# The first layer's weight tiles move from ahead of the working buffers in SBUF to behind them

## The chip, the cores and the metric

The kernel runs on one core of one Trainium2 chip. The metric is the device time of one execution in microseconds (us); for several executions the median is given. TensorE is PE in the profile, its weight loads stand apart as PEld; VectorE is DVE, ScalarE is ACT, GpSimd is POOL, and SyncE (SP) issues most of the DMAs.

## The reference

A dynamic convolution is followed by two feed-forward layers, all in float32, on 2 x 4096 tokens of 192 channels:

```python
w = softmax(weight_gen)                              # 8 heads, 7 taps for each token
x = einsum('bshk,bskhg->bshg', w, windows_of_7(x))   # 24 channels in a head
x = leaky(x.reshape(8192, 192) @ w_in1) @ w_out1     # 192 -> 2048 -> 192, leaky = max(0.01 h, h)
out = relu(x @ w_in2) ** 2 @ w_out2                  # 192 -> 2048 -> 192
```

## The kernel before, in words

**Tiling and order.** The tokens go in 16 blocks (tb) of 512. A phase is one layer l on one block. The five phases (0,0) to (0,4) come first, then (1,0), (0,5), (1,1), (0,6) and so on in turn up to (0,15), and last (1,11) to (1,15) of the second layer alone (L679 to L683). A phase has eight steps j, each for 256 of the 2048 hidden channels. So there are 256 steps, 128 of each layer. In a step TensorE runs `mm1(l, tb, j)` and then `mm2` of the step before the last one (LAG = 2): in the first two steps of a phase, `mm2` still belongs to the phase before, mostly to the other layer.

**The matmuls.** Values and weights are split in a high and a low float32r part, and the products high x high, high x low and low x high are added. Every matmul takes 64 partitions of contraction and 512 columns; two of them, one on partitions 0 to 63 and one on 64 to 127 (`HALVES`), are issued one behind the other and run side by side. `mm1` (L550) is 18 matmuls, nine such pairs: weights `wi0h`, `wi0l` (layer 0) or `wi1h`, `wi1l` (layer 1), moving tiles `xah`, `xbh`, `xsh`, `xal`, `xbl`, `xsl`. `mm2` (L592) is 20 matmuls, ten pairs: weights `wo0` or `wo1` (the trace calls both `wo`), moving tiles `gh` and `gl`, sums in the PSUM tiles `pa` and `pb`. A step thus has 19 pairs. The instructions of the two layers have the same shapes and the same waits.

**Other engines.** After `mm1`, ScalarE makes `gh` and `g` from PSUM (layer 0: two Prelu, L567 and L568, both read from PSUM; layer 1: a Relu from PSUM and two Square, L570 to L572), and VectorE makes `gl = g - gh` (L575). At a phase's end `total` (L613, L616) adds up the PSUM sums, and only then may the next phase's `mm2` write them. VectorE also does the convolution (`local_sum`, L472 and L484) ahead of a layer 0 phase, and at the start it decodes both layers' weights out of the words that lie in HBM (`piece`, L291 to L344).

**The planner.** `Plan.issue` writes out the order of each engine's operations from their costs and priorities. It knows tiles as rings of buffers, and nothing of addresses.

**Where tiles lie.** Pools are laid one behind the other in each SBUF partition in the order in which they are opened. Sizes follow from the tiles' shapes (bytes of one partition); places are counted from the start of `wi0h`:

| pool | what | bytes | place before |
|---|---|---|---|
| `const` | `ident`, `perm`, `warm`, then `wi0h`, `wi0l` (12,288 each), `wo0` (24,576) | 49,152 for layer 0's weights | 0 to 49,152 |
| `sb` | all working buffers; moving tiles of matmuls are `x..` (three rings of six tiles, 2,048 each), `gh`, `gl` (4,096 each) | 113,280 | 49,152 to 162,432 |
| `sg`, later `const2` | staging of layer 0's weights; in the same place, once that is done, layer 1's `wi1h`, `wi1l`, `wo1` | 49,152 | 162,432 to 211,584 |

Inside `sb`, the first `x` tile lies 25,216 bytes from the pool's start, the first `gh` 37,504, the first `gl` 53,888; all the moving tiles lie a multiple of 512 bytes from one another. One weight load takes 512 bytes of each partition, at a multiple of 512 bytes from the start of its layer's weights.

Of the kernel before, what the change touches and what calls it, by code (L numbers as in the profile page):

```python
# [141 lines left out]
def kernel(  # L142
# [42 lines left out]

    const = ctx.enter_context(tc.tile_pool(name="const", bufs=1))
    sb = ctx.enter_context(tc.tile_pool(name="sb", bufs=2))
    dram = ctx.enter_context(tc.tile_pool(name="dram", bufs=2, space=bass.MemoryType.DRAM))
    ps = ctx.enter_context(tc.tile_pool(name="ps", bufs=2, space=bass.MemoryType.PSUM))

# [27 lines left out]
    def weight_tiles(pool, l):  # L218
        wi.append({k: pool.tile([P, 3, NPR, P], F32R, name=f"wi{l}{k}") for k in "hl"})
        wo.append(pool.tile([P, NFC, 2 * D], F32R, name=f"wo{l}"))  # L220

    warm = const.tile([P, 1], F32, name="warm")
    weight_tiles(const, 0)
    wi_b = [[None] * NPR for _ in range(2)]
    wo_b = [[None] * NPR for _ in range(2)]
    SW = 2 * 3 * P
# [541 lines left out]
```

## Time and profile before

| what | value |
|---|---|
| median of 3 runs | 1188.23 us (1186.67 to 1189.9) |
| the profiled execution: its own time | 1187.0 us |
| its span, first to last instruction | 1185.2 us |
| mean granted clock of TensorE in it | 0.991 |
| busy: PE, PEld | 96%, 78% of the span |
| busy: ACT, DVE | 63%, 61% |

The profile shows one execution. Busy shares say little here by themselves; starts of consecutive matmuls, read from the timeline, say how long a step takes. A phase or a step is measured from the start of its first `mm1` matmul to that of the next.

### The profile page before, as it was taken

The page shows a single profiled execution, that of the slowest core. Times are in us where ns is not written, and L with a number is a line of the kernel's source. Part 1 is how long each engine was busy: PE and PEld are TensorE (multiplying, and loading weights), DVE is VectorE, ACT ScalarE, POOL GpSimd, SP SyncE. Part 2 cuts the span into 40 slices and gives each one's busy share as a digit, 9 for nine tenths or more (in the row PEclk, how much of TensorE's full clock was granted, in tenths as well). Part 3 has the DMA queues.
Part 4 walks back from the last instruction along what each step waited for, and adds up shares of the span by engine and source line. Part 5 has one row for each costly group of instructions (what it writes and reads, how often), then busy time and mean ns, then how long its engine had stood idle before and what let it go on. Part 6 is the DMA issues. An engine that isn't in the chain of part 4 may idle for free.

```text
span 1185.2 us, 22999 instructions
## 1 busy us (share of the span) xinstructions
PE 1137.3 (96%) x9748; PEld 929.3 (78%) x9748; DVE 725.5 (61%) x871; ACT 749.0 (63%) x830; POOL 15.9 (1%) x20
## 2 busy tenths in 40 slices
PE   2699999999999999999999999999999999999997
PEld 1479887888888888888888888888888888888885
DVE  7999999848465474745648475564846543344333
ACT  2555566574756748575674857657575675777774
POOL 0210000000000000000000000000000000000000
PEclk9799999999999999999999999999999999999999
DMA  8954646051512214142131513214151231121111
GB/s 185 221 105 105 158 129 171 14 136 19 148 20 79 70 42 127 19 124 44 57 93 37 131 19 105 60 33 121 22 146 19 86 80 45 56 63 37 19 19 18
DMA packets 112798, 94.29 MB, mean 80 GB/s; under 512 B 59644, under 2 KB 89114, under 8 KB 112696
## 3 DMA queue, kind: packets, MB, share of 16 engines
q1 hardware_dynamic: 108712, 87.99, 29.6%
q0 software_dynamic: 3792, 4.72, 2.5%
q8 instruction: 76, 1.25, 0.5%
q14 instruction: 26, 0.21, 0.1%
q10 hardware_dynamic: 192, 0.11, 0.0%
HBM read 50.06 MB, written 20.19 MB: 59 GB/s over the span
## 4 chain that ended last, share of the span: by engine, by line
PE 91%; DVE 6%; issue 1%; ACT 1%; DMA 1%; SPq 0%; POOL 0%; DVEq 0%; POOLq 0%; ACTq 0%
PE ph L550 43%; PE pa L592 29%; PE pb L592 19%; DVE gl L575 1%; DVE tmp L472 1%; DVE att L484 1%; DVE wa L302 1%; DVE wu L312 0%; DVE wu L308 0%; DVE wa L296 0%; DVE wo L344 0%; DMA xc<-in_x_dram 0%; ACT gh L567 0%; ACT wu L291 0%; DMA bw<-ob 0%
## 5 line engine op out<-in xcount | busy, mean ns | idle before, releaser
L575 DVE TENSOR_TENSOR gl<-g,gh 128x1024 fp32r<-128x1024 f32 x256 | 312.8, 1223 | 389.9 <-ACT g L572 293.1
L567 ACT ACTIVATE gh<-ph 128x1024 fp32r<-128x1024 f32 x128 | 131.6, 1028 | 262.8 <-PE ph L550 262.8
L592 PE MATMUL pa<-gh,wo 64*128 64x512 f32 x2048 | 280.9, 392 | 2.6 <-DVE s L616 2.0
L592 PEld LDWEIGHTS pa<-gh,wo 64*128 64x128 f32 x2048 | 194.2, 185 | 48.7 <-DVE oa L616 3.7
L570 ACT ACTIVATE g<-ph 128x1024 f32<-128x1024 f32 x128 | 131.7, 1029 | 120.6 <-PE ph L550 120.6
L592 PE MATMUL pa<-gl,wo 64*128 64x512 f32 x1024 | 160.7, 390 | 0.0
L592 PE MATMUL pb<-gh,wo 64*128 64x512 f32 x1024 | 160.4, 389 | 0.3 <-DVE wo L344 0.3
L592 PE MATMUL pb<-gl,wo 64*128 64x512 f32 x1024 | 160.5, 389 | 0.0
L571 ACT ACTIVATE gh<-g 128x1024 fp32r<-128x1024 f32 x128 | 135.8, 1061 | 4.0
L572 ACT ACTIVATE g<-g 128x1024 f32<-128x1024 f32 x128 | 136.0, 1062 | 3.5
L568 ACT ACTIVATE g<-ph 128x1024 f32<-128x1024 f32 x128 | 130.6, 1020 | 0.0
L592 PEld LDWEIGHTS pb<-gh,wo 64*128 64x128 f32 x1024 | 97.7, 185 | 21.3 <-DVE wo L344 0.7
L592 PEld LDWEIGHTS pb<-gl,wo 64*128 64x128 f32 x1024 | 97.7, 185 | 20.8
L592 PEld LDWEIGHTS pa<-gl,wo 64*128 64x128 f32 x1024 | 97.5, 184 | 20.9 <-DVE gl L575 0.4
L472 DVE TENSOR_TENSOR tmp<-xc,wg 128x768 f32<-128x768 f32 x96 | 91.1, 950 | 0.0
L484 DVE TENSOR_TENSOR att<-att,tmp 128x768 f32<-128x768 f32 x91 | 86.9, 955 | 1.7
L550 PE MATMUL ph<-xah,wi0h 64*128 64x512 f32 x256 | 53.0, 403 | 8.3 <-ACT wi0h L334 8.3
L550 PE MATMUL ph<-xah,wi0l 64*128 64x512 f32 x256 | 52.9, 402 | 3.3 <-DVE wi0l L344 3.3
L550 PE MATMUL ph<-xbl,wi0h 64*128 64x512 f32 x256 | 52.5, 399 | 1.0 <-DVE xbl L407 1.0
L550 PE MATMUL ph<-xsh,wi0l 64*128 64x512 f32 x256 | 52.8, 401 | 0.0
L550 PE MATMUL ph<-xsh,wi0h 64*128 64x512 f32 x256 | 52.5, 399 | 0.0
L550 PE MATMUL ph<-xbh,wi0l 64*128 64x512 f32 x256 | 52.5, 398 | 0.0
(98 smaller groups left out, 1462.2 us busy)
## 6 DMA issues: line engine op xcount, KB each, us to landing
xc<-in_x_dram SPq DMA_DIRECT2D x62, 240.0 KB, 4.5
xsh<-xah SPq DMA_DIRECT2D x60, 128.0 KB, 2.4
xsl<-xal SPq DMA_DIRECT2D x60, 128.0 KB, 2.4
raw<-in_moe_w_in_dram SPq DMA_DIRECT2D x32, 192.0 KB, 6.1
raw<-in_moe_w_out_dram SPq DMA_DIRECT2D x7, 768.0 KB, 5.1
sc<-xb SPq DMA_DIRECT2D x14, 384.0 KB, 2.3
ka<-s SPq DMA_DIRECT2D x16, 256.0 KB, 2.0
kb<-s SPq DMA_DIRECT2D x16, 256.0 KB, 3.2
```

Of the source, the lines that this page charges most:

```text
L302: lambda: nc.vector.scalar_tensor_tensor(I(wa), I(wu), SIGN, I(wa), op0=ALU.bitwise_and, op1=ALU.bitwise_or),
L472: nc.vector.tensor_tensor(dst, xk, wg.t[:, :, :, k : k + 1].to_broadcast([P, TB, H, G]), op=ALU.mult)
L484: lambda tmp=tmp: nc.vector.tensor_tensor(acc(), acc(), tmp.t, op=ALU.add),
L550: nc.tensor.matmul(ph.t[:, d, :], lhsT=w[HALVES[d], c, j, :], rhs=xs[s + hl].t[HALVES[d]], start=(i == 0), stop=(i == len(terms) - 1),)
L567: pl.op("ACT", W, pr, [ph], [gh], lambda: nc.scalar.activation(gh.t, ph.t, AF.Prelu, alpha=0.01))
L568: pl.op("ACT", W, pr, [ph], [g], lambda: nc.scalar.activation(g.t, ph.t, AF.Prelu, alpha=0.01))
L570: pl.op("ACT", W, pr, [ph], [g], lambda: nc.scalar.activation(g.t, ph.t, AF.Relu))
L571: pl.op("ACT", W, pr, [g], [gh], lambda: nc.scalar.activation(gh.t, g.t, AF.Square))
L572: pl.op("ACT", W, pr, [g], [g], lambda: nc.scalar.activation(g.t, g.t, AF.Square))
L575: lambda: nc.vector.tensor_tensor(gl.t, g.t, gh.t.bitcast(F32), op=ALU.subtract),
L592: nc.tensor.matmul(acc[d][w == "b"].t, lhsT=wt[:, {"ah": slice(0, P), "b": slice(P, 2 * P), "al": slice(2 * P, 3 * P)}[w]], rhs=g.t[HALVES ...
```

## The change

A pool `first` is opened behind `sb`, and layer 0's weight tiles are taken from it instead of from `const`. Nothing else is edited.

```diff
     const = ctx.enter_context(tc.tile_pool(name="const", bufs=1))
     sb = ctx.enter_context(tc.tile_pool(name="sb", bufs=2))
+    first = ctx.enter_context(tc.tile_pool(name="first", bufs=1))
     dram = ctx.enter_context(tc.tile_pool(name="dram", bufs=2, space=bass.MemoryType.DRAM))
...
     warm = const.tile([P, 1], F32, name="warm")
-    weight_tiles(const, 0)
+    weight_tiles(first, 0)
```

By the sizes above the working buffers then lie at 0 to 113,280, layer 0's weights at 113,280 to 162,432, and layer 1's weights where they were, at 162,432.

## Rows read from the trace of the kernel before

**Rows 1.** The page's part 1: busy us, share of the span, instructions.

```profile
PE 1137.3 (96%) x9748; PEld 929.3 (78%) x9748; DVE 725.5 (61%) x871; ACT 749.0 (63%) x830; POOL 15.9 (1%) x20
```

**Rows 2.** The page's part 4, the chain that ended last, by line.

```profile
PE ph L550 43%; PE pa L592 29%; PE pb L592 19%; DVE gl L575 1%; DVE tmp L472 1%; DVE att L484 1%; DVE wa L302 1%; DVE wu L312 0%; DVE wu L308 0%; DVE wa L296 0%; DVE wo L344 0%; DMA xc<-in_x_dram 0%; ACT gh L567 0%; ACT wu L291 0%; DMA bw<-ob 0%
```

**Rows 3.** Waits of PE from 82 us on: us in total, times, longest.

```profile
PE pa L592 <- DVE s L616: 2.0, 2, 1.1
PE ph L550 <- DVE xbl L407: 1.0, 1, 1.0
```

**Rows 4.** Windows: length, busy us (instructions) of PE, PEld, DVE, ACT, POOL, clock, DMA.

```profile
131.84:189.23 57.39, 57.39 (x496) 49.07 (x494) 53.42 (x65) 35.81 (x42) 0.00 (x0) 1.00 0.60 154
189.23:227.22 37.99, 35.95 (x307) 28.40 (x304) 35.28 (x47) 21.27 (x25) 0.00 (x0) 1.00 0.32 86
227.22:261.87 34.65, 34.65 (x306) 28.50 (x304) 18.84 (x21) 26.89 (x29) 0.00 (x0) 1.00 0.42 115
261.87:999.21 737.34, 737.34 (x6386) 598.37 (x6384) 427.89 (x496) 466.80 (x512) 0.00 (x0) 1.00 0.28 70
402.26:437.77 35.51, 35.51 (x306) 28.52 (x304) 27.13 (x33) 17.94 (x21) 0.00 (x0) 1.00 0.10 18
...
963.61:999.21 35.60, 35.60 (x306) 28.43 (x304) 14.67 (x16) 18.65 (x22) 0.00 (x0) 1.00 0.23 53
1033.86:1137.22 103.36, 103.36 (x915) 85.42 (x912) 42.22 (x45) 80.19 (x83) 0.00 (x0) 1.00 0.17 34
```

**Rows 5.** Line L550: duration of one matmul in ns, least, median, most; first and last start.

```profile
L550 PE MATMUL ph<-xsh,wi0l x256: 387/392/625, 28.8 to 996.4; 64*128 64x512 f32 x128
...
L550 PE MATMUL ph<-xah,wi1h x256: 386/386/394, 227.2 to 1167.4; 64*128 64x512 f32 x128
```

**Rows 6.** Timeline of PE: where `mm1` and `mm2` of four steps begin.

```profile
380.73 0.39 PE L550 MATMUL ph<-xah,wi1h 64*128 64x512 f32 x2
...
382.76 1.07 PE L592 MATMUL pa<-gh,wo 64*128 64x512 f32 x8
...
385.03 0.39 PE L550 MATMUL ph<-xah,wi1h 64*128 64x512 f32 x2
...
424.52 0.40 PE L550 MATMUL ph<-xah,wi0h 64*128 64x512 f32 x2
...
426.62 1.08 PE L592 MATMUL pa<-gh,wo 64*128 64x512 f32 x8
...
428.94 0.39 PE L550 MATMUL ph<-xah,wi0h 64*128 64x512 f32 x2
...
372.01 0.39 PE L550 MATMUL ph<-xah,wi1h 64*128 64x512 f32 x2
...
374.07 1.10 PE L592 MATMUL pa<-gh,wo 64*128 64x512 f32 x8
...
376.41 0.39 PE L550 MATMUL ph<-xah,wi1h 64*128 64x512 f32 x2
...
402.26 0.40 PE L550 MATMUL ph<-xah,wi0h 64*128 64x512 f32 x2
...
404.37 1.09 PE L592 MATMUL pa<-gh,wo 64*128 64x512 f32 x8
...
406.69 0.40 PE L550 MATMUL ph<-xah,wi0h 64*128 64x512 f32 x2
```

**Rows 7.** Timeline of the third step of a layer 0 phase.

```profile
411.12 0.41 PE L550 MATMUL ph<-xah,wi0h 64*128 64x512 f32 x2
411.12 0.19 PEld L550 LDWEIGHTS ph<-xbh,wi0h 64*128 64x128 f32 x2
...
413.27 0.53 PEld L592 LDWEIGHTS pa<-gh,wo 64*128 64x128 f32 x6 [0.34 <-DVE oa L616]
...
415.70 0.39 PE L550 MATMUL ph<-xah,wi0h 64*128 64x512 f32 x2
```

**Rows 8.** Waits of DVE from 82 to 227 us: us in total, times, longest.

```profile
DVE gl L575 <- PE pb L592: 5.9, 6, 1.9
```

## The prediction

> **What bounds the kernel now.** I read the page's busy shares first: PE is busy for 1137.3 of 1185.2 us [rows 1]. The chain that ended last says the same: L550 and L592 hold 91% of it [rows 2]. Third, the waits: from 82 us on PE waits for others for 3.0 us in three places [rows 3]; what comes before 82 us is the decoding of weights, where PE is not the bound. So from there to the end the time is the number of steps by the length of a step, and the only question is how long TensorE takes for a pair of matmuls.
>
> That length is not the same for the two layers. In the stretch of pure layer 1 at the end, 24 steps take 103.36 us [rows 4], 4.307 us each; divided by 19 pairs that is 226.7 ns for a pair. In the stretch of pure layer 0 near the start, 13 steps take 57.39 us, 4.415 us each or 232.3 ns for a pair. [...]
>
> The timeline says what it goes with [rows 6]. Where both weights are layer 1's, nine pairs of `mm1` take 2.03 us and ten of `mm2` 2.27. Where both are layer 0's, 2.10 and 2.32. In the second step of a layer 1 phase, `mm1` reads `wi1` and takes 2.06, while `mm2` still reads `wo0` and takes 2.34. So within one step, under the same ACT and DVE work, the length follows the weights that are read. One case fits less well: in the first step of a layer 0 phase `mm2` reads `wo1` and yet takes 2.32, after a slow `mm1`. In the case before, `mm1` was slower than 2.03 too after a slow `mm2`; I read both as a delay that takes some pairs to die out.
>
> Instructions and waits of the layers are alike, so what differs is where the weights lie. Every weight load begins while the matmul before it streams (both at 411.12 us [rows 7]): two reads of the same partitions at once. Layer 0's weights lie at multiples of 512 bytes from their start, the moving tiles at 49,152 + 25,216 = 145 x 512 + 128, so 128 bytes past such a multiple; layer 1's at 162,432 = 317 x 512 + 128, the same 128 past. In layer 1, all 256 matmuls of a kind take 386 to 394 ns, in layer 0 the median is 392 and none is below 387 [rows 5], whatever j or ring is read. So neither the row of the weight tile nor the ring of `x` counts. What remains is the place within 512 bytes, or the region of the partition as a whole. I take the first.
>
> **The change part by part.** No instruction is added, removed or moved in any queue, SP's and POOL's among them, and no wait: the planner does not see addresses, and `first` is opened as early as `const` was, so nothing waits for its space. The staging pool and layer 1's weights stay in their place. DMA issues and the cover of every DMA stay as they are. Two things move.
>
> Layer 0's weights go to 113,280 = 221 x 512 + 128, the moving tiles to 25,216 = 49 x 512 + 128. Now both layers' weights lie as layer 1's did to the moving tiles, and I price a pair at 226.7 ns throughout. No row shows weights in that region; the bounds are what rows 4 show, 226.7 and 232.3 ns, and nothing lower is known.
>
> The working buffers move down by 49,152 = 96 x 512 bytes. For layer 1's matmuls the place within 512 stays equal, so I take 0; the outer bound is that they take layer 0's 232.3 ns (a rival below).
>
> *The sum.* From 261.87 to 999.21 us there are 21 phases, 11 of layer 0 and 10 of layer 1, 168 steps in 737.34 us [rows 4]. At 4.307 us they take 723.6. Not all of the difference comes: in the third step of a layer 0 phase `mm2` waits until VectorE has read the old sums [rows 7]. That wait starts with the end of the `mm2` before, so a faster `mm1` only waits longer: 413.27 - 411.12 = 2.15 stays, against 2.04, and `mm2` at 2.43 keeps the 0.10 that it has over 2.32 to 2.34. So 0.21 x 11 = 2.3 us stay, and the stretch takes 725.9: **11.4 us gained**. The phase after it, like the one from 227.22 us (34.65 us against 8 x 4.307 = 34.46), gains 0.2, and that one 0.2. Between 189.23 and 227.22 us, about six of the eight steps are free of waits and gain 0.11 each, 0.7. The pure layer 1 steps gain 0.
>
> From 82 to 189 us, 24 steps of layer 0 could give 24 x 0.11 = 2.6 us. But DVE is busy for 53.42 of 57.39 us there [rows 4], in an order fixed by the planner, and at its end PE waits 1.0 us for `xbl` and twice for DVE's sums [rows 3]. A faster PE mostly waits longer there: what is late next is DVE. It does not get nothing, since DVE itself waits 5.9 us for PE's `mm2` in this stretch [rows 8]. Bounds 0 and 2.6; I take 0.5, nearer to the row of a full DVE. Before 82 us nothing.
>
> Sum: 11.4 + 0.4 + 0.7 + 0.5 = **13.0 us**. The profiled execution took 1187.0 us (span 1185.2), so 1174.0; it lies 1.2 us under the median of the runs, 1188.23, from which the same gain gives 1175.2. I say 1175.0. ACT and DVE do not become the bound: in the steady phases the fuller of them is busy for 27.13 of 35.51 us [rows 4].
>
> [...]
>
> **The rivals.**
> *No change (chance 0.10).* The place does not matter; layer 0 is slow by its own nature, as by ACT's two reads of PSUM beside TensorE's writes, or the move cures layer 0 and hurts layer 1 equally. For it: `wo1` at 2.32 in the first step of a layer 0 phase [rows 6]. Against: `wo0` at 2.34 under layer 1's ACT work. Time 1187.0, by the median 1188.
>
> *Slower (0.08).* What counts is the region: a read from the lowest 49,152 bytes delays the pair. Before, these hold layer 0's weights; after, working buffers, which both layers read. Layer 0 keeps its time, and layer 1's 128 steps go from 4.307 or 4.33 to 4.42: 88 steps beside layer 0 by 0.11 and 40 at the end by 0.115, 14.3 us, so 1201.3, by the median 1202.5. The last pure layer 1 stretch decides: 128 x 19 = 2,432 pairs outweigh the gain when each loses over 13.0 / 2,432 = 5.3 ns. For it: layer 1's weights, the fast ones, lie highest. Against: the `x` rings lie all over the buffers, and layer 1 takes 386 ns with every one [rows 5].
>
> *Half (within faster, 0.12).* Only `mm1` or only `mm2` of layer 0 is cured, each about half of the 0.11 us in a step: 6.5 us, 1181.7 by the median.
>
> **How the numbers follow.** Full cure 0.70 and half 0.12 make faster 0.82; no change 0.10; slower 0.08. A measurement of this kernel tells about 0.3%, 3.6 us, from no change. The full cure alone reaches from 1171 (the fastest run less 13.0 and less the 2.1 us more that the early stretch could give, 1171.6) to 1178 (the slowest run less 12.5, 1177.4). The range takes in the half cure, up to 1184, and begins at 1170.
>
> **What would show it.** Right: layer 0's matmuls have a median of 386 ns on L550; a pure layer 0 step without waits takes 4.31 us; the stretch of 21 phases takes about 726 us; the last stretch of layer 1 is unchanged at 4.307 a step; the wait in the third step grows by 0.06 us; PE's waits between 82 and 227 us grow from 3.0 to about 5. Wrong: layer 0's pairs still at 232 ns (no change), or layer 1's last stretch above 4.307 (the region counts). If layer 0's pairs are fast and the time hardly falls, DVE in the early stretch took more than I gave it.

## The result and the profile after

The median is 1173.58 us (1172.23 to 1177.38, 4 runs) against 1188.48 us before (1186.67 to 1189.9, 4 runs). The ratio is 0.9883, with a 95% interval of 0.9867 to 0.99: faster by 14.9 us, by the interval between 11.9 and 15.8 us. Forecast were 13.0.

The profiled execution of the changed kernel took 1177.38 us with a span of 1175.6; it is the slowest of the four, which matters below. Its line numbers are one higher, so L550 is now L551 and L592 is L593. First the windows over the same stretches as in [rows 4], found by the same first matmuls, with the same columns: 13 steps of pure layer 0, the last phase of layer 0 at the start, the first phase of layer 1, the 21 phases, and 24 steps of pure layer 1.

```profile
135.60:191.58 55.98, 55.98 (x496) 46.27 (x494) 53.18 (x65) 35.77 (x42) 0.00 (x0) 1.00 0.61 158
191.58:229.08 37.50, 35.09 (x308) 28.33 (x305) 35.06 (x47) 21.28 (x25) 0.00 (x0) 1.00 0.32 87
229.08:263.53 34.45, 34.45 (x307) 28.47 (x304) 19.01 (x21) 26.89 (x29) 0.00 (x0) 1.00 0.43 118
263.53:989.78 726.25, 726.25 (x6386) 597.14 (x6384) 427.18 (x496) 466.48 (x512) 0.00 (x0) 1.00 0.28 71
1024.23:1127.60 103.37, 103.37 (x916) 85.43 (x913) 42.21 (x45) 80.19 (x83) 0.00 (x0) 1.00 0.17 34
```

Layer 0's step is 55.98 / 13 = 4.306 us, layer 1's 103.37 / 24 = 4.307, and the granted clock is 1.00 in all rows, as in [rows 4]. The 21 phases went from 737.34 to 726.25 us. Second, line L551, durations of one matmul as in [rows 5]:

```profile
L551 PE MATMUL ph<-xsh,wi0l x256: 386/386/626, 29.0 to 987.1; 64*128 64x512 f32 x128
...
L551 PE MATMUL ph<-xah,wi1h x256: 386/386/386, 229.1 to 1157.7; 64*128 64x512 f32 x128
```

Both layers have a median of 386 ns now; before, layer 0 had 392 in the kind shown and 388 to 395 in its other kinds. Third, the timeline of PE, a step at the start of a layer 1 phase (376.00 on; both products fit now) and the third step of a layer 0 phase, which [rows 7] showed before (410.45 on):

```profile
376.00 0.39 PE L551 MATMUL ph<-xah,wi1h 64*128 64x512 f32 x2
...
378.04 1.07 PE L593 MATMUL pa<-gh,wo 64*128 64x512 f32 x8
...
380.30 0.39 PE L551 MATMUL ph<-xah,wi1h 64*128 64x512 f32 x2
...
410.45 0.39 PE L551 MATMUL ph<-xah,wi0h 64*128 64x512 f32 x2
...
412.61 1.20 PE L593 MATMUL pa<-gh,wo 64*128 64x512 f32 x8
...
415.00 0.39 PE L551 MATMUL ph<-xah,wi0h 64*128 64x512 f32 x2
...
412.60 0.30 PEld L593 LDWEIGHTS pa<-gh,wo 64*128 64x128 f32 x4 [0.38 <-DVE oa L617]
```

In the first, `mm1` takes 2.04 and `mm2` 2.26 us. In the second, `mm1` still takes 2.16, since `mm2` waits for VectorE's read of the old sums (its first weight load, the last line, waits 0.38 us; before, 0.34 [rows 7]), and `mm2` takes 2.39. Last, PE's waits from 82 us on, as in [rows 3], and under them DVE's own from 82 to 229 us, as in [rows 8]:

```profile
PE pa L593 <- DVE s L617: 2.5, 2, 1.3
PE pt L393 <- DVE xal L408: 1.9, 1, 1.9
PE ph L551 <- DVE xbl L408: 1.1, 1, 1.1
```

```profile
DVE gl L576 <- PE pb L593: 6.9, 6, 2.1
```

PE waits 5.5 us for DVE where it waited 3.0, but the two sums do not hold the same waits. The one for `xal`, 1.9 us, comes just ahead of the second block's first step. The kernel before has it too, 1.22 us long, and there it ends at 81.14 us, just ahead of the 82 us from which [rows 3] counts:

```profile
81.14 0.51 PE L392 MATMUL pt<-xah,perm 128*128 128x512 f32 x1 [1.22 <-DVE xal L407]
```

Without it, 3.0 became 3.6 us.

**Where the time went, in these two executions.** The second block's first step (step 8 of 256) began at 81.8 us before and at 84.3 after, 2.5 us later, and it took 4.52 us before and 6.62 after, 2.1 us longer. Windows of that step and of the 23 steps behind it, up to the start of the fifth block, first of the kernel before:

```profile
81.81:86.33 4.52, 4.52 (x39) 3.70 (x40) 4.45 (x6) 3.02 (x4) 0.00 (x0) 1.00 0.00 0
86.33:189.23 102.90, 101.99 (x876) 92.08 (x874) 95.99 (x117) 59.64 (x71) 0.00 (x0) 1.00 0.52 131
```

and of the changed kernel, with the first 4 us of step 8 in a row of their own:

```profile
84.34:88.35 4.01, 4.01 (x21) 3.12 (x20) 3.94 (x6) 1.07 (x2) 0.00 (x0) 0.50 0.00 0
84.34:90.96 6.62, 6.62 (x39) 5.38 (x40) 4.78 (x6) 3.02 (x4) 0.00 (x0) 0.64 0.00 0
90.96:191.58 100.62, 99.40 (x876) 88.82 (x874) 94.93 (x116) 59.65 (x71) 0.00 (x0) 1.00 0.53 134
```

In the changed kernel the granted clock was 0.50 in the first 4 us of this step, after PE had waited 1.9 us for `xal`; before, it was 1.00. Behind the step it is 1.00 in both kernels. There 102.90 became 100.62, then 37.99 became 37.50, 34.65 became 34.45 twice, and the 21 phases gained 11.1: 14.3 us in all. Less the 4.6 us lost up to the end of step 8, that is 9.6 us, which is 1187.0 less 1177.38. The 4.6 us are no part of the change: over these two executions and one of each of the ten experiments, step 8 begins anywhere from 81.2 to 84.3 us and takes 4.44 to 4.56 us at a clock of 1.00, or 5.44 to 6.62 at 0.64 to 0.82. The five with the lower clock are two kernels whose tiles fit (the changed one and the first experiment) and three whose tiles do not all fit.

### The profile page after: what moved, and what is told of

The parts are those of the page before. It is cut to its first block, busy times and chain, and to the rows that moved or that the text cites. A ratio compares the mean times of both kernels' runs of the same rounds, so it can differ in the third digit from the quotient of the medians.

```text
span 1175.6 us, 22999 instructions
## 1 busy us (share of the span) xinstructions
PE 1125.3 (96%) x9748; PEld 926.9 (79%) x9748; DVE 724.4 (62%) x871; ACT 748.6 (64%) x830; POOL 15.8 (1%) x20
## 4 chain that ended last, share of the span: by engine, by line
PE 91%; DVE 6%; issue 1%; ACT 1%; DMA 1%; SPq 0%; POOL 0%; DVEq 0%; POOLq 0%; ACTq 0%
PE ph L551 43%; PE pa L593 29%; PE pb L593 19%; DVE gl L576 1%; DVE tmp L473 1%; DVE att L485 1%; DVE wa L303 0%; DVE wu L309 0%; DVE wu L313 0%; DVE wa L297 0%; DMA xc<-in_x_dram 0%; DMA wg<-in_weight_gen_dram 0%; DVE wo L345 0%; ACT g L569 0%; ACT gh L568 0%
## 5 line engine op out<-in xcount | busy, mean ns | idle before, releaser
L593 PE MATMUL pa<-gh,wo 64*128 64x512 f32 x2048 | 277.5, 389 | 3.1 <-DVE s L617 2.5
L593 PEld LDWEIGHTS pa<-gh,wo 64*128 64x128 f32 x2048 | 193.3, 185 | 47.3 <-DVE oa L617 4.1
L593 PE MATMUL pb<-gh,wo 64*128 64x512 f32 x1024 | 158.5, 387 | 0.2 <-DVE wo L345 0.2
L593 PE MATMUL pa<-gl,wo 64*128 64x512 f32 x1024 | 158.2, 386 | 0.0
L593 PE MATMUL pb<-gl,wo 64*128 64x512 f32 x1024 | 158.1, 386 | 0.0
L593 PEld LDWEIGHTS pb<-gh,wo 64*128 64x128 f32 x1024 | 96.9, 185 | 20.3 <-DVE wo L345 0.7
L593 PEld LDWEIGHTS pa<-gl,wo 64*128 64x128 f32 x1024 | 96.6, 184 | 19.9 <-DVE gl L576 0.4
L593 PEld LDWEIGHTS pb<-gl,wo 64*128 64x128 f32 x1024 | 96.7, 184 | 19.4
L551 PE MATMUL ph<-xah,wi0h 64*128 64x512 f32 x256 | 52.0, 400 | 7.8 <-ACT wi0h L335 7.8
L551 PE MATMUL ph<-xah,wi0l 64*128 64x512 f32 x256 | 51.9, 399 | 3.4 <-DVE wi0l L345 3.4
L551 PE MATMUL ph<-xbl,wi0h 64*128 64x512 f32 x256 | 51.5, 396 | 1.1 <-DVE xbl L408 1.1
L551 PE MATMUL ph<-xsh,wi0h 64*128 64x512 f32 x256 | 51.4, 395 | 0.0
L551 PE MATMUL ph<-xsh,wi0l 64*128 64x512 f32 x256 | 51.4, 395 | 0.0
L551 PE MATMUL ph<-xal,wi0h 64*128 64x512 f32 x256 | 51.4, 395 | 0.0
```

The costliest lines, as they stand in the source:

```text
L551: nc.tensor.matmul(ph.t[:, d, :], lhsT=w[HALVES[d], c, j, :], rhs=xs[s + hl].t[HALVES[d]], start=(i == 0), stop=(i == len(terms) - 1),)
L593: nc.tensor.matmul(acc[d][w == "b"].t, lhsT=wt[:, {"ah": slice(0, P), "b": slice(P, 2 * P), "al": slice(2 * P, 3 * P)}[w]], rhs=g.t[HALVES ...
```

## The experiments

The trace shows no addresses: all distances are worked out from the order of the pools and the sizes of the tiles. The theory is that TensorE is delayed when a weight tile does not lie at the same place within some hundreds of bytes as the moving tiles ("fits" below); the rival is that the region of the partition counts. In all windows below, where nothing else is said, the first row is 13 steps of pure layer 0 and the last 24 steps of pure layer 1, with the columns of [rows 4].

**Fit in the old region.** The kernel before, with one 128-byte tile put ahead of layer 0's weights instead of behind them:

```diff
     warm = const.tile([P, 1], F32, name="warm")
+    mx_t = const.tile([P, R, 1], F32, name="mx_t")
     weight_tiles(const, 0)
...
-        mx = pl.buf(sb, [P, R, 1], F32, "mx", "mx", 1)
+        mx = Buf(lambda i: mx_t, ("mx", 1))
```

> The kernel before, with its 128-byte tile mx taken out of the working buffers and put ahead of layer 0's weights. The weights stay ahead of the working buffers, but now lie at the same place within 512 bytes as the moving tiles; every moving tile and layer 1's weights keep their addresses. Theory (the place of weights against moving tiles within 512 bytes counts): a pure layer 0 step takes 4.31 us, the 21 phases 726 us, the time 1174 (1171 to 1178), as after the change. Rival (the region counts): a layer 0 step stays at 4.42, the time at 1188.

Measured: 1175.31 us (4 runs) against 1191.09 (7 runs), ratio 0.9877 (0.9853 to 0.9901). Windows, the middle row being the 21 phases:

```profile
133.57:189.55 55.98, 55.98 (x496) 46.27 (x494) 53.16 (x65) 35.79 (x42) 0.00 (x0) 1.00 0.61 158
261.50:987.76 726.26, 726.26 (x6386) 597.15 (x6384) 427.17 (x496) 466.31 (x512) 0.00 (x0) 1.00 0.28 71
1022.22:1125.58 103.36, 103.36 (x915) 85.42 (x912) 42.22 (x45) 80.18 (x83) 0.00 (x0) 1.00 0.17 34
```

The whole gain is there, with layer 0's weights still ahead of the working buffers, 128 bytes from where they were. The region does not count here (55.98 / 13 = 4.306 us a step of layer 0, as in the changed kernel); the order of the pools was only the means.

**Misfit in the new region.** The changed kernel, with the 896-byte tile `wg` behind the working buffers. All weights stay; the moving tiles shift by 896 = 3 x 256 + 128 bytes.

```diff
     sb = ctx.enter_context(tc.tile_pool(name="sb", bufs=2))
+    tail = ctx.enter_context(tc.tile_pool(name="tail", bufs=1))
...
-        wg = pl.buf(sb, [P, TB, H, K], F32, "wg", "wg", 1)
+        wg = pl.buf(tail, [P, TB, H, K], F32, "wg", "wg", 1)
```

> The changed kernel, with the 896-byte tile wg taken from the front of the working buffers and put behind them. All weights keep the addresses of the changed kernel; the moving tiles shift down by 896 bytes, so both layers' weights lie 128 bytes short of them within 512, as layer 0's did before. Theory: both layers' steps take 4.42 us, the last pure stretch of layer 1 too; against the changed kernel 13 us are lost on layer 0 and 128 x 0.11 = 14 on layer 1, 1201 us (1196 to 1206). Rival (the region counts, or the address of the weights alone): 1174, steps of 4.31.

Measured: 1202.73 us (4 runs), ratio to the kernel before 1.0113 (1.0081 to 1.0144).

```profile
135.25:192.64 57.39, 57.39 (x496) 46.48 (x494) 53.44 (x65) 35.69 (x42) 0.00 (x0) 1.00 0.60 154
265.86:1009.52 743.66, 743.66 (x6386) 599.83 (x6384) 427.81 (x496) 466.64 (x512) 0.00 (x0) 1.00 0.28 70
1044.83:1150.81 105.98, 105.98 (x915) 85.82 (x912) 42.27 (x45) 80.19 (x83) 0.00 (x0) 1.00 0.16 33
```

Read the last row against the 103.37 us of the changed kernel: layer 1, whose weights did not move, takes 105.98 / 24 = 4.416 us a step, while layer 0 took 4.306 in the experiment above. So neither the layer, nor the address of the weights alone, nor ACT's reads of PSUM makes a step slow. This is the slow rival's price, reached by a misfit.

**Control for it.** `mx` goes behind the working buffers as well, so that the moving tiles move by 1,024 bytes.

```diff
-        wg = pl.buf(sb, [P, TB, H, K], F32, "wg", "wg", 1)
-        mx = pl.buf(sb, [P, R, 1], F32, "mx", "mx", 1)
+        wg = pl.buf(tail, [P, TB, H, K], F32, "wg", "wg", 1)
+        mx = pl.buf(tail, [P, R, 1], F32, "mx", "mx", 1)
```

> Control for the run with wg behind the working buffers: wg and mx both lie there, so the moving tiles move down by 1024 bytes, a multiple of 256, against the changed kernel. Theory: 4.31 us a step in both layers and 1174 us (1171 to 1178). Were wg's new place itself the cause of that run's loss, 1201 again.

Measured: 1172.64 us (one run, the kernel before beside it 1191.52).

```profile
130.81:186.80 55.99, 55.99 (x497) 46.27 (x494) 53.15 (x65) 35.78 (x42) 0.00 (x0) 1.00 0.60 157
258.77:985.05 726.28, 726.28 (x6386) 597.14 (x6384) 427.00 (x496) 466.42 (x512) 0.00 (x0) 1.00 0.28 71
1019.50:1122.86 103.36, 103.36 (x914) 85.42 (x912) 42.20 (x45) 80.17 (x83) 0.00 (x0) 1.00 0.17 34
```

Fast in both layers: not `wg`'s new place, but the 128 bytes.

**How far off is slow?** Four kernels give each layer its own distance, by unused bytes ahead of its weights, and by `mx` behind the working buffers for another 128; a fifth shifts the weights inside a tile. The edits for 32 and 64 (the others have other sizes):

```diff
     sb = ctx.enter_context(tc.tile_pool(name="sb", bufs=2))
+    pad0 = ctx.enter_context(tc.tile_pool(name="pad0", bufs=1)).tile([P, 8], F32, name="pad0")
     first = ctx.enter_context(tc.tile_pool(name="first", bufs=1))
...
+    pad1 = ctx.enter_context(tc.tile_pool(name="pad1", bufs=1)).tile([P, 8], F32, name="pad1")
     stage = ExitStack()
```

and for 16 and 48 (where the 8 columns, 32 bytes, by which layer 0's tile is longer put the second 32 further):

```diff
-        wi.append({k: pool.tile([P, 3, NPR, P], F32R, name=f"wi{l}{k}") for k in "hl"})
-        wo.append(pool.tile([P, NFC, 2 * D], F32R, name=f"wo{l}"))
+        o, c = ((4, 4)[l], 3 * NPR * P)
+        w = pool.tile([P, 4 * c + 8], F32R, name=f"w{l}")
+        cut = lambda i: w[:, o + i * c : o + (i + 1) * c].rearrange("p (s q m) -> p s q m", s=3, q=NPR)
+        wi.append({k: cut(i) for i, k in enumerate("hl")})
+        wo.append(w[:, o + 2 * c : o + 4 * c].rearrange("p (f e) -> p f e", f=NFC))
```

> The changed kernel with 32 unused bytes ahead of layer 0's weights and 32 more ahead of layer 1's: layer 0's weights lie 32 bytes past the moving tiles' place within 512, layer 1's 64 past. Theory says only that steps move off 4.31 us where the place counts in units of 32 or 64 bytes: up to 4.42 a step, up to 1200 us. If the place counts in units of 128 bytes alone, both stay at 4.31 and the time at 1174.

> The changed kernel with mx moved behind the working buffers and 128 unused bytes ahead of layer 1's weights: layer 0's weights lie 128 bytes past the moving tiles' place within 512, layer 1's 256 past. If the slow case is any misfit of 128, both layers take 4.42 us a step, 1201 us; if it repeats every 256 bytes, layer 1 stays at 4.31 and layer 0 takes 4.42, 1188 us; if only weights short of the moving tiles are slow, both stay at 4.31, 1174 us.

> The changed kernel with 96 unused bytes ahead of layer 0's weights and 64 more ahead of layer 1's: layer 0's weights lie 96 bytes past the moving tiles' place within 256, layer 1's 160 past. Theory, after 32, 64 and 128 were slow: both layers at 4.41 to 4.43 us a step, 1201 us. Rival (some other place is as good as 0, or better): a layer at 4.31 or less, 1188 or less.

> The changed kernel with mx behind the working buffers, 64 unused bytes ahead of layer 0's weights and 32 more ahead of layer 1's: layer 0's weights lie 192 bytes past the moving tiles' place within 256, layer 1's 224 past. Theory: both layers at 4.41 to 4.43 us a step, 1201 us. Rival: a layer at 4.31 or less, 1188 or less.

> The changed kernel with each layer's weights in one tile and shifted in it by 16 bytes: layer 0's weights lie 16 bytes past the moving tiles' place within 256, layer 1's 48 past. Theory: 48 is slow as 32 and 64 are, 4.43 us a step; 16 tells whether the good place is one point (layer 0 at 4.41 to 4.43, 1201 us) or a stretch of over 16 bytes (layer 0 at 4.31, 1188 us).

Measured, one run each: 1202.36, 1187.9, 1203.46, 1193.78 and 1200.3 us in that order, the kernel before beside them at 1191.09 (median of 7) for the first two and 1187.15 (one run) for the others. The windows, a fence for each kernel in the same order:

```profile
132.27:189.90 57.63, 57.63 (x496) 46.40 (x494) 53.50 (x65) 35.74 (x42) 0.00 (x0) 1.00 0.60 154
1045.05:1151.45 106.40, 106.40 (x915) 85.88 (x912) 42.27 (x45) 80.19 (x82) 0.00 (x0) 1.00 0.16 33
```

```profile
132.83:190.22 57.39, 57.39 (x496) 46.48 (x494) 53.44 (x65) 35.80 (x42) 0.00 (x0) 1.00 0.59 154
1034.77:1138.13 103.36, 103.36 (x914) 85.42 (x912) 42.21 (x45) 80.17 (x83) 0.00 (x0) 1.00 0.17 34
```

```profile
131.56:189.43 57.87, 57.87 (x496) 46.53 (x494) 53.54 (x65) 35.73 (x42) 0.00 (x0) 1.00 0.58 152
1046.17:1152.57 106.40, 106.40 (x916) 85.58 (x913) 42.30 (x45) 80.14 (x82) 0.00 (x0) 1.00 0.16 33
```

```profile
130.64:187.18 56.54, 56.54 (x497) 46.35 (x494) 53.28 (x65) 35.80 (x42) 0.00 (x0) 1.00 0.60 157
1036.46:1142.86 106.40, 106.40 (x914) 85.31 (x912) 42.33 (x45) 80.13 (x82) 0.00 (x0) 1.00 0.16 33
```

```profile
134.11:191.74 57.63, 57.63 (x496) 48.25 (x494) 53.50 (x65) 35.69 (x42) 0.00 (x0) 1.00 0.60 153
1042.96:1149.36 106.40, 106.40 (x915) 86.34 (x913) 42.25 (x45) 80.17 (x82) 0.00 (x0) 1.00 0.16 33
```

First rows divided by 13, second by 24, give the step in these pure stretches for each distance (0 is the changed kernel):

| weights past the moving tiles, bytes | 0 | 16 | 32 | 48 | 64 | 96 | 128 | 160 | 192 | 224 | 256 |
|---|---|---|---|---|---|---|---|---|---|---|---|
| step, us | 4.307 | 4.433 (but see below) | 4.433 | 4.433 | 4.433 | 4.452 | 4.415 | 4.433 | 4.349 | 4.433 | 4.307 |

256 is as good as 0, and in these stretches nothing between is; 192 is the least bad. At 256, in layer 1 of the second kernel, moving tiles and weights both lie 128 bytes from their places within 256 in the changed kernel: the distance counts, not the place of either. Of the expectations, 192 met neither side, since it is neither slow in full nor a fit, and 32, 64 and 96 (4.433 and 4.452) came out a little slower than the most that was given. No distance is better than 0, so no kernel here beats the changed one by its layout.

At 16 bytes the pure stretch is not the whole story. Here are the last five steps of two layer 0 phases of that kernel, (0,5) and (0,6):

```profile
278.50:300.67 22.17, 22.17 (x192) 17.91 (x190) 19.87 (x22) 9.72 (x10) 0.00 (x0) 1.00 0.12 22
349.40:370.95 21.55, 21.55 (x194) 17.80 (x191) 19.85 (x22) 9.72 (x10) 0.00 (x0) 1.00 0.12 20
```

The layout and the clock are the same and the work of the other engines is alike, and yet a step takes 4.434 us in the first and 4.310, a fit's time, in the second. By the starts in the trace, four of the 11 layer 0 phases among the 21, (0,6), (0,8), (0,10) and (0,12), end fast, and seven slow; each keeps to its way from `mm2` of the third step on, which waits for VectorE (0.34 us before [rows 7], 0.38 in the changed kernel). In the first two steps of all 11, `mm1` takes 2.04 us, as in a fit, behind an `mm2` of 2.33. So 16 bytes off can be as slow as 64 or as fast as 0; what decides between them, no run here shows.

**Half a fit.** In the changed kernel with `mx` behind the working buffers, unused bytes between `wi` and `wo` let only `wo0` and `wi1` fit:

```diff
         wi.append({k: pool.tile([P, 3, NPR, P], F32R, name=f"wi{l}{k}") for k in "hl"})
+        pool.tile([P, 16 if l else 32], F32, name=f"gap{l}")
         wo.append(pool.tile([P, NFC, 2 * D], F32R, name=f"wo{l}"))
```

> The changed kernel with mx behind the working buffers, so that the input weights wi0 lie 128 past the moving tiles' place, and 128 unused bytes ahead of wo0 and 64 ahead of wo1, so that wo0 and wi1 lie at it and wo1 64 past. Theory: each product follows its own weights: pure layer 0 steps take 2.09 + 2.27 = 4.36 us, pure layer 1 steps 2.04 + 2.33 = 4.37, with some pairs of delay carried over; each half is worth about half of the 0.11, 1189 us in all. Rival (a step as a whole is slow once any of its weights misfit): 4.42 and more in both, 1201 us.

Measured: 1195.62 us (one run), the kernel before beside it 1187.15. The windows, and the timeline of PE over one step of layer 0 and one of layer 1:

```profile
133.82:191.37 57.55, 57.55 (x496) 46.43 (x494) 53.46 (x65) 35.82 (x42) 0.00 (x0) 1.00 0.60 154
1039.39:1144.99 105.60, 105.60 (x914) 85.73 (x912) 42.27 (x45) 80.18 (x82) 0.00 (x0) 1.00 0.17 33
```

```profile
151.53 0.41 PE L553 MATMUL ph<-xah,wi0h 64*128 64x512 f32 x2
...
153.64 1.09 PE L595 MATMUL pa<-gh,wo 64*128 64x512 f32 x8
...
155.96 0.40 PE L553 MATMUL ph<-xah,wi0h 64*128 64x512 f32 x2
...
1052.60 0.39 PE L553 MATMUL ph<-xah,wi1h 64*128 64x512 f32 x2
...
1054.66 1.10 PE L595 MATMUL pa<-gh,wo 64*128 64x512 f32 x8
...
1056.99 0.39 PE L553 MATMUL ph<-xah,wi1h 64*128 64x512 f32 x2
```

`mm2` of layer 0 fits and yet takes 2.32 us, behind a slow `mm1` (2.11). `mm1` of layer 1 fits and takes 2.06, behind a slow `mm2` (2.33). In the changed kernel, where both products fit, they take 2.26 and 2.04. That `wo0` fits is seen in the first two steps of the layer 1 phases among the 21, which read `wi1` and `wo0`: they take 4.31 us. So here a slow product hands its delay on, for most of the nine or ten pairs of the next; in the kernel with 16 bytes, above, it did not. Neither expectation held: the theory's 4.36 and 4.37 us a step were too low (4.43 and 4.40), and the rival's "4.42 and more in both" was too high for layer 1.

**Which reads have to fit?** Here every weight tile fits the moving tiles of its own product, but `x` lies 128 bytes off `gh` and `gl`. A weight load runs beside the matmul ahead of it (both begin at 411.12 us in [rows 7]), so the reads that run at the same time misfit only where the product changes, twice in a step.

```diff
-    first = ctx.enter_context(tc.tile_pool(name="first", bufs=1))
+    first, tail, gp, first_o = (
+        ctx.enter_context(tc.tile_pool(name=n, bufs=1)) for n in ("first", "tail", "gp", "first_o")
+    )
...
-        wi.append({k: pool.tile([P, 3, NPR, P], F32R, name=f"wi{l}{k}") for k in "hl"})
-        wo.append(pool.tile([P, NFC, 2 * D], F32R, name=f"wo{l}"))
+        wo.append((pool if l else first_o).tile([P, NFC, 2 * D], F32R, name=f"wo{l}"))
+        if l:
+            pool.tile([P, 32], F32, name="gap")
+        wi.append({k: pool.tile([P, 3, NPR, P], F32R, name=f"wi{l}{k}") for k in "hl"})
...
-        mx = pl.buf(sb, [P, R, 1], F32, "mx", "mx", 1)
+        mx = pl.buf(tail, [P, R, 1], F32, "mx", "mx", 1)
...
-        g = pl.buf(sb, [P, 2, N], F32, "g", "g", 2)
-        gh = pl.buf(sb, [P, 2, N], F32R, "gh", "gh", 3)
-        gl = pl.buf(sb, [P, 2, N], F32R, "gl", "gl", 2)
+        g = pl.buf(gp, [P, 2, N], F32, "g", "g", 2)
+        gh = pl.buf(gp, [P, 2, N], F32R, "gh", "gh", 3)
+        gl = pl.buf(gp, [P, 2, N], F32R, "gl", "gl", 2)
```

> The changed kernel, relaid so that every weight tile fits the moving tiles of its own product within 256 bytes (wi0, wi1 with x; wo0, wo1 with gh and gl), while x lies 128 bytes off gh and gl: mx is the spacer behind wi0, gh, g and gl have a pool of their own behind it, and wo1 lies ahead of wi1 with 128 unused bytes between. A weight load runs beside the matmul before it, so at the two places in a step where the product changes, the tile that streams and the weights that are loaded do not fit; elsewhere they do. Theory (what counts is the pair of reads that run at the same time): steps between 4.31 and 4.42 us, some 4.36, with a few slow pairs behind each of the two places, 1187 us (1178 to 1197). Rival (what counts is a weight tile against its own product's moving tile): 4.31 in both layers, 1174. Second rival (all tiles must fit each other): 4.42 throughout, 1201.

Measured: 1177.27 us (one run, the kernel before beside it 1191.52). The timeline of PE over a step of pure layer 1, in part:

```profile
1053.79 0.39 PE L555 MATMUL ph<-xah,wi1h 64*128 64x512 f32 x2
1054.03 0.39 PE L555 MATMUL ph<-xbh,wi1h 64*128 64x512 f32 x2
...
1055.61 0.40 PE L555 MATMUL ph<-xsl,wi1h 64*128 64x512 f32 x2
1055.84 1.07 PE L597 MATMUL pa<-gh,wo 64*128 64x512 f32 x8
...
1058.12 0.39 PE L555 MATMUL ph<-xah,wi1h 64*128 64x512 f32 x2
```

A step takes 1058.12 - 1053.79 = 4.33 us, 0.02 over the fit. By the starts of all pairs in the trace, the 0.02 sits where the product changes and nowhere else: from the last `x` matmul to the first `gh` matmul 232 to 233 ns instead of 226.7, the next interval 230 to 231, and the same behind the last `gl`; all others are 226 or 227. That is the place at which the load of the next product's weights runs beside a stream that it does not fit (in the trace of the changed kernel the first load for an `mm2` and the last `x` matmul ahead of it both begin at 407.96 us). Here `x` and `gh` lie apart too, so this run alone does not tell weights from moving tiles; but in the kernel before, where all moving tiles fit one another, the same interval, from the last `gl` matmul of a layer 1 phase to the first `x` matmul with `wi0`, is 232 to 233 ns as well. The rival by which only a weight's own moving tile counts would have given 4.31, and all tiles fitting each other 4.42. The theory's place is right and its size, 4.36, was too big: one misfit costs about 10 ns and dies out in one pair here.

## Why the prediction was right, and where not

- **The clue** held: layer 0 was slow by where its weights lay, not by what the layer does. The misfit in the new region shows it from the other side, since it slows layer 1 from 4.307 to 4.416 us a step. One reading behind it was too sharp: that no layer 0 matmul takes less than 387 ns is true of the kind in [rows 5], but two other kinds go down to 384 and 385.
- **Place within 512 bytes, not the region:** right between the two, but the period is 256 bytes (4.307 us a step at 256 bytes off as at 0); the trace of before, with distances of 0 and 128 alone, could not tell that from 512. The 128 bytes that the prediction worked out were the whole matter.
- **The step of 4.307 us for layer 0:** measured 4.306. The 21 phases: 725.9 forecast, 726.25 measured.
- **The wait that stays in the third step:** 2.15 forecast for `mm1`, 2.16 measured; `mm2` 2.37 forecast (2.27 + 0.10), 2.39 measured. The wait itself grew from 0.34 to 0.38 us, where 0.06 us more was forecast, and keeps 11 x 0.2 us of the gain.
- **The early stretch** is the term that was mis-sized, and its reason failed. Of 24 x 0.11 = 2.6 us the prediction took 0.5, because DVE is nearly full there and a faster PE would mostly wait. But in the very row that it cites, 57.39 us became 55.98: all 13 steps gained in full, with PE busy throughout. Behind step 8 the 23 steps gained 2.3 us, near the upper bound, and PE's waits grew by 0.6 us in all, not by 2. That their sum came to 5.5 us, forecast about 5, was luck: a wait of 1.9 us had moved across the edge of the window. Over all 24 steps this pair shows a gain of only 0.2 us (107.42 to 107.24), since step 8 ran in part at the lower clock (0.64 over the step); in the control with both `wg` and `mx` moved, whose step 8 had a clock of 1.00, the 24 steps took 105.1. DVE's own waits for PE's `mm2`, the reason given for not taking 0, did not shrink: 6.9 us after, 5.9 before [rows 8].
- **The total:** 13.0 forecast, 14.9 by the medians with an interval of 11.9 to 15.8, and 14.3 in the profiled pair behind step 8. Of the 1.3 us between 13.0 and 14.3, the early stretch gives 1.8 and the later terms take back 0.5.
- **The half rival failed.** It priced a fit of one product at half of the gain. In the run with half a fit a slow product slows the next: with `wo0` alone cured, layer 0 took 4.43 us a step in its pure stretch, against 4.415 with no cure. The other half, `wi` alone cured, was tried only on layer 1 at 64 bytes: 4.400 against 4.433, about a quarter of the loss. This also accounts for the row that fitted badly, `wo1` at 2.32 us in [rows 6]: it is the same 2.32 as `wo0`'s there, a fitting product behind a slow one.
- **The rival of no change failed.** In the pure stretches TensorE waits for no other engine, PE being busy for 57.39 of 57.39 us [rows 4], and yet its pairs come later when weights and moving tiles do not fit: by 4.415 - 4.307 = 0.108 us in 19 pairs, 5.7 ns each.

Left open: why 256 bytes, why 192 costs a third of what its neighbours do (0.042 us a step against 0.126), why 16 bytes off is slow in some phases and not in others, and how long a delay lives on. Nothing here looks into that.

## What to carry to other kernels

Where a kernel is bound by matmuls with a new weight load each, compare the interval between their starts across stages: if it differs at the same granted clock (here 226.7 against 232.3 ns, both at 1.00), look at where weights and moving tiles lie. Place both at the same address modulo 256 bytes: in the pure stretches of this kernel a step took 4.307 us at 0 and at 256 bytes off and 4.349 to 4.452 at the nine distances tried between, 128 bytes in the place of one layer's weights were worth 1.2%, and a misfit in both layers cost 1.1% against the kernel before. Let all products that follow one another fit, since a slow one can slow the next (a `wo0` that fits took 2.32 us behind a slow `mm1`, and 2.26 behind one that fits).

## What was not expected of the hardware

A pair of 64-partition float32r matmuls of 512 columns comes every 226.7 ns when the operands fit, and every 229 to 234 ns at the nine other distances tried (4.349 to 4.452 us in 19 pairs), with 16 bytes off as bad as 64 there, but without any loss in the last five steps of four later phases. In the kernel with half a fit and the one with `x` and `g` apart, the interval at a given place in the step repeats to within a nanosecond or two; in kernels with all reads of a layer 128 bytes off, intervals in a pure stretch go from 228 to 241 ns. Over one execution of each of the twelve kernels, the start, while weights are decoded, varies by 3 us (step 8 at 81.2 to 84.3 us) and step 8 by another 2.2 with the granted clock, while the 21 phases agree to 0.03 us in three kernels whose tiles fit (726.25, 726.26, 726.28).
